# Delta rule and a rational mixture layer on one Trainium2 core: keys and queries transposed on TensorE in float32, weight words converted 768 at a time

## The chip, the core and the metric

The kernel runs on one core of one Trainium2 chip. The metric is the device time of one launch in microseconds (us). A core has five engines with an instruction stream each: TensorE (PE, the matmuls; PEld is its weight loads), VectorE (DVE), ScalarE (ACT), GpSimd (POOL) and SyncE (SP), which here does little but issue DMAs. Every engine works its stream in order and waits on semaphores for the others.

## What is computed

The reference first runs a delta rule over 768 tokens for 4 x 8 heads of width 48. After that every token's 384 values pass a two-layer network whose activation is a quotient of two polynomials.

```
k_n = k / (norm(k) + 1e-06)
for t in range(S):
    y[:, :, t] = q[t] @ state
    v_old = state @ k_n[t]
    state = state + beta[t] * outer(k_n[t], v[t] - v_old)
x = y, laid out as (B * S, H * D) = 3072 x 384
h = x @ w_in                                   # 384 x 2048
P = a0 + a1*h + a2*h^2 + a3*h^3
Q = 1 + |b0|*|h| + |b1|*h^2
out = (P / (Q + 1e-06)) @ w_out                # 2048 x 384
```

The two weight matrices come as float64, that is as pairs of 32-bit words, and are turned into float32 on the chip.

## The kernel before

**Chunks.** Tokens are worked in 12 chunks of 64 tokens (`C`, `NCH`). In a chunk the 32 sequences (4 batches times 8 heads) are held as two pairs (`PAIRS`) times two blocks of 64 partitions. Every float32 factor of a matmul is split into a float16 high part and a float16 rest (`split16`: ACT writes the high part, DVE or POOL subtracts it), and a product is three float16 passes (`PASSES`, `mm3`).

**A chunk's attention** is cut into steps that different chunks are in at the same time. `ahead` (L948) loads keys, values and queries with SP DMAs (`load`, L110) and normalizes the keys (`keys_normalized`, L486). `front` (L915) writes the transposed keys on the block diagonal of `kbd` (`keys_transposed`, L506), multiplies keys with keys (`key_products`, tile `pg`, L510), inverts 16 x 16 blocks on DVE (`inverse`, L523), scales and transposes the queries (L634) and multiplies them with the keys (`query_products`, tile `pm`, L649). `middle` (L932) fills the other block-diagonal operands by DMA (`to_diagonal`, L422; `diagonals`, L640). `back` (L888) solves (`pu`), updates the state with the keys in token order (`knbd`, product `pd`, L700) and makes the outputs (L711).

**Transposing before.** `transposed` (L448) splits 128 x 768 float32 values with ACT (L226) and POOL (L230) into the one buffer `kn`. Two DMAs (L458) write both parts to DRAM (`xdk`, `xdq`), padded from 48 to 64 values. A transposing DMA (L475) reads them back as `tk` or `tq`. Only chunk 0 (`soon`) transposes on TensorE, in float16 (L468, copies L470). For the state update, four DMAs (L428) read `xdk` out of DRAM again in runs of 128 bytes into `knbd`. `kbd` and `qbd` are filled from all 64 partitions, padding too (L433).

**Weights before.** `to_f32` (L309) makes float32 of 256 words (`load_in`, L329: three calls for each of 8 units) or 192 words (`load_out`, L347: four calls for each unit): a DMA into one of nine staging tiles of tags `mw`, `mu`, `mr`; ACT takes the absolute value of the high words (L316) into `wao` or `wai`; POOL clamps it (L317); DVE shifts (L318) and merges sign and low bits with two `scalar_tensor_tensor` (L325). The result is split into float16: in `load_in` on ACT and DVE, in `load_out` one half on ACT and DVE and the other half on POOL and ACT (L366 to L371).

**The layer** is a loop of 96 units (8 of each chunk): `hidden` (18 matmuls, L808), `numerator` (three ACT and three DVE instructions, L826 to L833), `quotient` (two ACT, three DVE, one POOL, L841 to L847) and `accumulate` (12 matmuls, L862). `attention` (L959) puts one step of four later chunks beside each unit.

**What sets the order.** A scheduler fixes each engine's stream before the run by a simulated time line. `tc.high_priority` lifts the recurrent steps, and the unit's DVE instructions keep their order (`in_order`, L794). Nearly all DMAs share the one SP queue. PSUM tiles rotate in pools: `ps_f` has one buffer, which `pg`, `pm`, `pe`, `pfq` and, from chunk 3 on, `px` take in turn.

Of the kernel before, what the change touches and what calls it, by code (L numbers as in the profile page):

```python
# [36 lines left out]
def kernel(  # L37
# [35 lines left out]
        "kn": [P, NPAIR, 2, H, 2, DP],  # L73
# [33 lines left out]
    LD_BUFS = {"k": 1, "q": 1, "v": 2}  # L107
    loaded = {}

    def load(nm, c):  # L110
        t = sb.tile([P, NPAIR * H, D], F32, tag="ld" + nm, name=f"{nm}_{c}", bufs=LD_BUFS[nm])
        with behind(nm, c):
            for b in range(2):
                sl, src = slice(b * C, (b + 1) * C), SRC[nm][:, :, c * C : (c + 1) * C]
                if nm == "v":
                    nc.sync.dma_start(out=t[sl], in_=src[2 * b : 2 * b + 2].rearrange("p h t d -> t (p h) d"))
                else:
                    for i in range(2):
                        nc.sync.dma_start(out=t[sl, i * H : (i + 1) * H], in_=src[2 * i + b].rearrange("h t d -> t h d"))  # L119
        loaded[nm, c] = t  # L120
# [64 lines left out]
    kn_b = zeroed(1, [P, 2, H, 2, DP], F16, "kn", lambda t: t[:, :, :, :, D:DP])[0]  # L185
# [123 lines left out]
    def to_f32(t, src, nm, keep=MIN_NORMAL):  # L309
# [6 lines left out]
        nc.scalar.activation(a, wh.bitcast(F32), AF.Abs)  # L316
        nc.gpsimd.tensor_scalar(a, a, 3.0e38, keep, op0=ALU.min, op1=ALU.max)  # L317
        nc.vector.tensor_scalar(  # L318
            t, a.bitcast(U32), 3, KEEP, op0=ALU.logical_shift_left, op1=ALU.bitwise_and
        )  # L320
        for word, scalar, in1, op0, op1 in (
            (wh, 0xC0000000, t, ALU.bitwise_and, ALU.bitwise_or),
            (wl, 29, t, ALU.logical_shift_right, ALU.bitwise_or),
        ):
            nc.vector.scalar_tensor_tensor(out=t, in0=word, scalar=scalar, in1=in1, op0=op0, op1=op1)  # L325
# [3 lines left out]
    def load_in(i):  # L329
        w64 = moe_w_in.bitcast(U32)  # L330
        t = w_out[:, i].rearrange("p a b e -> p (a b e)").bitcast(U32).rearrange("p (c f) -> p c f", c=NCC)
        for cc in range(NCC):
            to_f32(t[:, cc], w64[cc * P : (cc + 1) * P, i * 4 * P : (i + 1) * 4 * P], f"i{i}_{cc}")
        s2 = w_in[:, i, 0].bitcast(BF16)
        nc.scalar.activation(s2, t.bitcast(F32), AF.Square)
# [9 lines left out]
        split16((w_in[:, i, 0], w_in[:, i, 1]), t.bitcast(F32), sw[:, 0, i : i + 1])  # L345

    def load_out(i):  # L347
        w64 = moe_w_out.bitcast(U32)
        if i + 1 < NU:
            to = w_out[:, i + 1].rearrange("p a b e -> p a (b e)").bitcast(U32)  # L350
            to = [to[:, j] for j in range(2)]
        else:
            to = [staged([P, DM], U32, f"wo32_{i}_{j}") for j in range(2)]
        fs = sb.tile([P, 2], F32, tag="wfs", name=f"wfs_{i}")
        for j in range(2):
            f = 2 * i + j
            for e in range(2):
                cl = slice(e * DM // 2, (e + 1) * DM // 2)
                to_f32(to[j][:, cl], w64[f * P : (f + 1) * P, e * DM : (e + 1) * DM], f"o{f}_{e}", gate)
            sum_squares(fs[:, j : j + 1], to[j].bitcast(F32), w_out[:, i, 0, j])  # L360
        ss = sb.tile([P, 2], F32, tag="ss", name=f"vss_{i}")
        nc.vector.tensor_scalar(ss[:, 0:1], fs[:, 0:1], fs[:, 1:2], 2.0 ** -30, op0=ALU.add, op1=ALU.max)
# [677 lines left out]
```

## Time and profile before

| what | value |
|---|---|
| time, median of 3 runs | 843.59 us (839.91 to 846.07) |
| the profiled execution's own time | 849.25 us |
| its span from first to last instruction | 845.5 us |
| mean granted TensorE clock | 0.944 of full speed |
| DMA packets, bytes | 466507, 111.46 MB |
| first unit's DVE work (L830) starts | 150.29 us |
| starts of chunks 1, 2, 3, 4, 5 of the layer | 223.66, 296.13, 371.55, 428.05, 483.62 us |
| starts of chunks 6 to 11 | 544.97, 604.99, 664.30, 719.16, 764.19, 800.18 us |

The span is 3.75 us shorter than the execution's time, and that execution was 5.66 us above the median of the runs. An engine's busy time counts an instruction that stands blocked in its execution as busy. Rows that group instructions give the line of kernel.py, the engine, the operation, output and inputs with shapes, the count, the busy time with the mean of one in ns, and then the idle time ahead of them with what ended it. A row of a view by stretches gives the stretch, its length, each engine's busy time with the count of instructions, then the granted clock, the mean busy share of the 16 DMA engines and GB/s.

### The profile page before, as it was taken

What the parts mean: (1) busy time and instruction counts of PE and PEld (TensorE: products, weight loads), DVE (VectorE), ACT (ScalarE), POOL (GpSimd) and SP (SyncE); (2) the same over time, 40 slices, a digit from 0 to 9 for tenths busy, and PEclk for the clock granted to TensorE, in tenths of its full rate; (3) what the DMA queues carried; (4) which work ended last, traced back from release to release, by engine and by line L of the source; (5) the groups of instructions that cost most, each with busy time, mean ns of one, the idle gap of its engine ahead of it and who ended that gap; (6) DMA issues with size and microseconds to landing.
All of it is one profiled execution on the core that took longest, in us unless ns stands there. A gap on an engine that the chain in (4) does not pass through costs nothing.

```text
span 845.5 us, 23179 instructions
## 1 busy us (share of the span) xinstructions
PE 627.7 (74%) x9264; PEld 493.8 (58%) x9264; DVE 740.2 (88%) x1405; ACT 617.1 (73%) x1278; POOL 338.1 (40%) x322
## 2 busy tenths in 40 slices
PE   0330346778778777866978988789789789999995
PEld 0220344666566666755866866667567667786662
DVE  5999896688879778987998999989988799998996
ACT  4866658768667675866966968768668768788873
POOL 6545754334435333253433433432433332222232
PEclk9999996898989898989999999989899999999999
DMA  8998979769979879999599399696597674300000
GB/s 237 249 212 170 225 155 170 123 140 169 157 130 165 146 120 191 146 140 183 93 145 187 71 176 150 119 193 105 98 167 111 110 103 80 76 2 21 1 19 19
DMA packets 466507, 111.46 MB, mean 132 GB/s; under 512 B 431328, under 2 KB 463072, under 8 KB 466400
## 3 DMA queue, kind: packets, MB, share of 16 engines
q1 hardware_dynamic: 464224, 108.83, 71.3%
q8 instruction: 72, 1.18, 0.6%
q10 hardware_dynamic: 2176, 1.17, 0.5%
q14 instruction: 35, 0.29, 0.1%
HBM read 40.47 MB, written 26.23 MB: 79 GB/s over the span
## 4 chain that ended last, share of the span: by engine, by line
DVE 34%; PE 19%; DMA 17%; SPq 11%; ACT 10%; issue 7%; POOL 1%; ACTq 0%; DVEq 0%; POOLq 0%
PE ph L808 7%; PE po L862 5%; DVE ph L845 4%; DVE w_out L325 4%; DVE mg L844 3%; DVE mw L830 3%; DVE mu L833 3%; DVE mu L832 3%; SPq L119 3%; PE pu L401 2%; DMA tq<-xdq 2%; DMA gd<-g 2%; DMA tk<-xdk 2%; SPq L475 2%; DVE mu L846 2%
## 5 line engine op out<-in xcount | busy, mean ns | idle before, releaser
L862 PE MATMUL po<-w_out,mg 128*128 128x384 f16 x1152 | 226.5, 339 | 33.3 <-DVE mg L844 20.9
L847 POOL TENSOR_TENSOR mg<-mu,mr 128x512 f16<-128x512 f32 x96 | 124.8, 1300 | 258.1 <-DVE mu L846 203.8
L808 PE MATMUL ph<-xT,w_in 128*128 128x256 f16 x1728 | 216.3, 280 | 14.1 <-DVE mu L846 11.2
L808 PEld LDWEIGHTS <-w_in 128*128 128x128 f16 x1728 | 169.8, 101 | 51.1 <-DVE mu L846 14.4
L862 PEld LDWEIGHTS <-mg 128*128 128x128 f16 x1152 | 109.5, 101 | 103.4 <-DVE mg L844 27.7
L401 PEld LDWEIGHTS <-kbd 128*128 128x128 f16 x1680 | 66.7, 109 | 47.8 <-issue 43.3
L830 DVE SCALAR_TENSOR_TENSOR mw<-mr,msc,ph 128x512 f32<-128x512 f32 x96 | 71.1, 741 | 22.1 <-ACT mu L828 21.9
L831 ACT ACTIVATE mw<-mw 128x512 f32<-128x512 f32 x96 | 60.4, 629 | 39.7 <-DVE mw L830 39.2
L845 DVE SCALAR_TENSOR_TENSOR ph<-mw,msc,mg 128x512 f32<-128x512 f32 x96 | 81.4, 848 | 1.0
L844 DVE SCALAR_TENSOR_TENSOR mg<-mu,msc,mr 128x512 f16<-128x512 f32 x96 | 81.1, 844 | 0.0
L826 ACT ACTIVATE mr<-ph,msc 128x512 f32<-128x512 f32 x96 | 65.2, 679 | 18.7 <-PE ph L808 6.9
L828 ACT ACTIVATE mu<-ph,coef,msc 128x512 f32<-128x512 f32 x96 | 74.2, 773 | 0.0
L846 DVE SCALAR_TENSOR_TENSOR mu<-mu,msc,ph 128x512 f32<-128x512 f32 x96 | 71.1, 741 | 1.4
L833 DVE SCALAR_TENSOR_TENSOR mu<-mu,msc,ph 128x512 f32<-128x512 f32 x96 | 70.7, 736 | 1.0
L841 ACT ACTIVATE mr<-mw,msc 128x512 f32<-128x512 f32 x96 | 69.2, 721 | 1.7
L401 PE MATMUL pu<-z,ebd 128*128 128x48 f16 x1728 | 54.9, 185 | 18.1 <-DVE z L232 13.5
L401 PEld LDWEIGHTS <-ebd 128*128 128x128 f16 x1728 | 53.9, 98 | 21.7 <-issue 19.4
L832 DVE TENSOR_TENSOR mu<-ph,mu 128x512 f32<-128x512 f32 x96 | 65.5, 682 | 0.0
L842 ACT ACTIVATE mr<-mr 128x512 f32<-128x512 f32 x96 | 60.3, 628 | 1.3
L401 PEld LDWEIGHTS <-wbd 128*128 128x128 f16 x1152 | 37.7, 99 | 35.9 <-issue 34.8
L230 POOL TENSOR_TENSOR mm<-m,mm 128x1024 f16<-128x1024 f32 x12 | 29.2, 2436 | 73.6 <-ACT mm L226 64.5
L401 PE MATMUL pm<-tq,kbd 128*128 128x64 f16 x576 | 27.0, 220 | 20.1 <-DMA tq<-xdq 18.3
(195 smaller groups left out, 1195.0 us busy)
## 6 DMA issues: line engine op xcount, KB each, us to landing
wsi<-in_moe_w_in_dram SPq DMA_DIRECT2D x24, 256.0 KB, 5.0
xdk<-kn SPq DMA_DIRECT2D x24, 256.0 KB, 3.7
kbd<-tk SPq DMA_DIRECT2D x24, 256.0 KB, 5.5
gd<-g SPq DMA_DIRECT2D x24, 256.0 KB, 3.5
wso<-in_moe_w_out_dram SPq DMA_DIRECT2D x32, 192.0 KB, 3.9
xdq<-kn SPq DMA_DIRECT2D x24, 256.0 KB, 3.6
mbd<-mm SPq DMA_DIRECT2D x24, 256.0 KB, 5.5
wc<-img SPq DMA_DIRECT2D x24, 256.0 KB, 5.1
```

Source lines behind the costliest of these rows:

```text
L401: nc.tensor.matmul(dst[p][:, h], head(bd, lp, p * H + h), head(rt, rp, p * H + h), start=start and n == 0 and h == 0, stop=stop and n == l ...
L808: nc.tensor.matmul(ph[:, i], w_in[:, f2, wp, cc, i * P : (i + 1) * P], x[:, xp, cc], start=k == 0, stop=k == 3 * NCC - 1,)
L828: nc.scalar.activation(u, ph, AF.Identity, scale=A3, bias=a2)
L830: in_order(nc.vector.scalar_tensor_tensor(out=w, in0=z, scalar=B0, in1=ph, op0=ALU.add, op1=ALU.mult))
L832: in_order(nc.vector.tensor_mul(u, ph, u))
L833: in_order(nc.vector.scalar_tensor_tensor(out=u, in0=u, scalar=A1, in1=ph, op0=ALU.add, op1=ALU.mult))
L841: nc.scalar.activation(r, w, AF.Ln, bias=Q0)
L844: in_order(nc.vector.scalar_tensor_tensor(out=g[:, 0], in0=u, scalar=A0, in1=r, op0=ALU.add, op1=ALU.mult))
L845: in_order(nc.vector.scalar_tensor_tensor(out=t, in0=w, scalar=Q0, in1=g[:, 0], op0=ALU.add, op1=ALU.mult))
L846: in_order(nc.vector.scalar_tensor_tensor(out=u, in0=u, scalar=A0, in1=t, op0=ALU.add, op1=ALU.subtract))
L847: nc.gpsimd.tensor_mul(g[:, 1], u, r)
L862: nc.tensor.matmul(po[p], g[:, gp, i, p * P : (p + 1) * P], w_out[:, f2, wp, i], start=f2 == lo and i == 0 and k == 0, stop=f2 == hi - 1 a ...
```

## The change

1. `load` puts keys and queries into two fixed tiles `kw`, `qw` of [128, 8, 2, 64] float32 whose padding is zeroed once. One partition's heads lie as TensorE wants them.
2. `transposed` makes 8 TensorE transposes of 128 x 128 in float32 into one `ps_f` tile (`pt`). Then `split16` writes high part and rest from PSUM for each pair: two ACT copies and two DVE subtractions of 128 x 512. This holds for keys and queries of all 12 chunks. The DRAM rows, the transposing DMAs and the float16 transposes of chunk 0 are gone, and queries are no longer split in SBUF.
3. Keys for the state update are still split by ACT and POOL, in two halves of 384, into one of three tiles `kn` in SBUF, which four DMAs copy to `knbd` in runs of 256 bytes. Chunk 11 skips this.
4. `kbd` and `qbd` are filled from 48 partitions instead of 64.
5. `to_f32` takes 768 words at a time, 16 calls instead of 56, in place in its target. Staging is three tiles of tag `mx`; a unit's `u`, `w`, `r` share such a tile.
6. In `load_out` both halves of `w_out` are split together by ACT and DVE; POOL no longer scales or subtracts there.
7. `dynamic_dma_scratch_size=2048` is given to the program.

```diff
-        t = sb.tile([P, NPAIR * H, D], F32, tag="ld" + nm, name=f"{nm}_{c}", bufs=LD_BUFS[nm])
+        t = wide[nm] if nm in wide else sb.tile([P, HP, D], F32, tag="ld" + nm, name=f"{nm}_{c}", bufs=LD_BUFS[nm])
...
-    kn_b = zeroed(1, [P, 2, H, 2, DP], F16, "kn", lambda t: t[:, :, :, :, D:DP])[0]
+    kn_b = zeroed(3, [P, 2, 2, NH, DP, HG], F16, "kn", lambda t: t[:, :, :, :, D:DP], eng=nc.vector)
...
-        nc.sync.dma_start(out=st.rearrange("p f w -> p (f w)"), in_=src)
+        parts_ = src.shape[1]
+        nc.sync.dma_start(out=st.rearrange("p (a f) w -> p a (f w)", a=parts_), in_=src)
...
+        to_f32(t, w64[:, i * 4 * P : (i + 1) * 4 * P].rearrange("(c p) x -> p c x", p=P), f"i{i}")
...
-        for j in range(2):
-            if j == 0:
-                split16((w_out[:, i, 0, j], w_out[:, i, 1, j]), to[j].bitcast(F32), ss[:, 1:2])
-            else:
-                scaled(to[j].bitcast(F32), ss[:, 1:2])
-                split16((w_out[:, i, 0, j], w_out[:, i, 1, j]), to[j].bitcast(F32), eng=nc.gpsimd)
+        split16((w_out[:, i, 0], w_out[:, i, 1]), t, ss[:, 1:2])
...
             if nm == "kn":
-                for a in range(HG):
+                for p in PAIRS:
                     nc.sync.dma_start(
-                        out=bd[sl].rearrange("t p i (n a) b d -> t (p i n) a b d", a=HG)[:, :, a, b],
-                        in_=t[:, :, :, :, a, b].rearrange("p i n t d -> t (p i n) d"),
+                        out=bd[sl, p, :, :, b].rearrange("t i n d a -> t (i n) (d a)"),
+                        in_=t[p * C : (p + 1) * C, b].rearrange("t i n d a -> t (i n) (d a)"),
                     )
...
-    def transposed(x, src, nm, soon):
+    def transposed(x, nm):
+        t = sb.tile([P, NPAIR, 2, NH, C, HG], F16, tag="tt", name="t" + nm)
+        pt = ps_f.tile([P, H, P], F32, tag="a", name=f"pt{nm}")
+        for h in range(H):
+            nc.tensor.transpose(pt[:, h], x[:, h].rearrange("p b d -> p (b d)"), identf)
         for p in PAIRS:
+            split16(
+                [t[:, p, i].rearrange("x n t a -> x n a t") for i in range(2)],
+                pt[:, :, p * C : (p + 1) * C].rearrange("x (n a) t -> x n a t", a=HG),
             )
+        return t
...
+        if c + 1 < NCH:
+            kd = kn_b[c % 3]
+            for b in range(2):
+                split16(
+                    [kd[:, b, i, :, :D].rearrange("p n d a -> p n a d") for i in range(2)],
+                    kt[:, :, b].rearrange("p (n a) d -> p n a d", a=HG),
+                    eng=nc.gpsimd,
+                )
+        info[c] = {"tk": transposed(wide["k"], f"k_{c}"), "kd": kd}
...
-        scaled(qt, d["sq"])
-        d["tq"] = transposed(kn_b, qt, f"q_{c}", c == 0)[0]
+        scaled(qt[..., :D], d["sq"])
+        d["tq"] = transposed(qt, f"q_{c}")
```

The change also lets the scheduler write other streams. DVE before, where the words of `w_out` begin (`wso` is a staged block of words, `wao` the clamped magnitudes):

```order
L318 TENSOR_SCALAR w_out_135<-wao0_1_1113 128x192
L318 TENSOR_SCALAR w_out_135<-wao1_0_1122 128x192
L325 SCALAR_TENSOR_TENSOR w_out_135<-wso0_1_1111,w_out_135 128x192
L325 SCALAR_TENSOR_TENSOR w_out_135<-wso1_0_1120,w_out_135 128x192
L325 SCALAR_TENSOR_TENSOR w_out_135<-wso0_1_1111,w_out_135 128x192
L318 TENSOR_SCALAR w_out_135<-wao1_1_1130 128x192
L325 SCALAR_TENSOR_TENSOR w_out_135<-wso1_0_1120,w_out_135 128x192
L325 SCALAR_TENSOR_TENSOR w_out_135<-wso1_1_1128,w_out_135 128x192
```

And the same place of the change:

```order
L316 TENSOR_SCALAR w_out_143<-w_out_143 128x768
L286 TENSOR_SCALAR tab_145<-tab_145,coef_103 128x4
L235 SCALAR_TENSOR_TENSOR w_in_142<-w_out_143,sw_144,w_in_142 128x768
L318 SCALAR_TENSOR_TENSOR w_out_143<-wso1_968,w_out_143 128x768
L351 TENSOR_SCALAR vss_0_959<-wfs_0_957 128x1
L318 SCALAR_TENSOR_TENSOR w_out_143<-wso1_968,w_out_143 128x768
L316 TENSOR_SCALAR w_out_143<-w_out_143 128x768
L254 TENSOR_SCALAR sw_144<-lgw0_961 128x1
```

Three instructions of 768 now stand where twelve of 192 stood. Of the 48 subtractions of the new transposes 10 come ahead of the first unit (keys of chunks 0, 1, 2 and queries of 0, 1), 38 behind it.

SP before, one round of the loop (the queue that issues DMAs; `xdq`, `xdk` are the DRAM rows):

```order
L458 DMA xdq_5702<-kn_109 64x8x256 x2
L433 DMA qbd_117<-tq_4594 64x16x128 x2
L441 DMA mbd_125<-mm_4821 64x16x128
L475 DMA_TRANSPOSE tq_5705<-xdq_5702 128x2048
L458 DMA xdk_5950<-kn_109 64x8x256 x2
L884 DMA out_dram<-ob_5967 64x2x384 x2
L441 DMA mbd_125<-mm_4821 64x16x128
L475 DMA_TRANSPOSE tk_5953<-xdk_5950 128x2048
L587 DMA img_129<-wh_6163 128x16x16
```

And SP of the change, where `qbd` of the same chunk is filled:

```order
L423 DMA kbd_121<-tk_4499 48x16x128 x2
L569 DMA wc_4723<-img_139 64x16x64 x2
L496 DMA gd_5178<-g_5228 64x16x64 x2
L418 DMA knbd_127<-kn_117 64x8x128 x4
L506 DMA gb_5331<-gd_5178 128x16x16
L423 DMA qbd_125<-tq_4242 48x16x128 x2
L122 DMA qw<-in_q_dram 64x8x48
```

Six issues a chunk are gone, and `knbd` reads `kn` in SBUF. TensorE's stream of the change, with the transposes of the queries of chunk 8 (`ptq`) ahead of a unit's first matmuls (`ph`):

```order
L391 LDWEIGHTS knbd_127
L391 MATMUL pd_7899<-z_7896,knbd_127 128x48
L443 MATMUL ptq_7576<-identf,qw 128x128 x8
L786 LDWEIGHTS w_in
L786 MATMUL ph_7601<-xT_7107,w_in 128x256
```

Before, nothing stood between `pd` and the unit's matmuls there; now whatever the eight transposes wait for, the unit behind them waits for too.

More of the change, by code (lines that the diff above doesn't have):

```diff
@@ L106 @@
     SRC = {"k": k, "q": q, "v": v}
-    LD_BUFS = {"k": 1, "q": 1, "v": 2}
+    LD_BUFS = {"v": 2}
     loaded = {}
+    wide = {nm: cpool.tile([P, H, 2, DP], F32, name=nm + "w") for nm in "kq"}
+    for t in wide.values():
+        nc.vector.memset(t[:, :, :, D:], 0.0)
     def load(nm, c):
-        t = sb.tile([P, NPAIR * H, D], F32, tag="ld" + nm, name=f"{nm}_{c}", bufs=LD_BUFS[nm])
+        t = wide[nm] if nm in wide else sb.tile([P, HP, D], F32, tag="ld" + nm, name=f"{nm}_{c}", bufs=LD_BUFS[nm])
         with behind(nm, c):
@@ L349, in load_out @@
         if i + 1 < NU:
-            to = w_out[:, i + 1].rearrange("p a b e -> p a (b e)").bitcast(U32)
-            to = [to[:, j] for j in range(2)]
-        else:
-            to = [staged([P, DM], U32, f"wo32_{i}_{j}") for j in range(2)]
-        fs = sb.tile([P, 2], F32, tag="wfs", name=f"wfs_{i}")
-        for j in range(2):
[L356 to L360, printed above, removed]
+            t = w_out[:, i + 1].rearrange("p a b e -> p (a b e)").bitcast(U32)
+        else:
+            t = staged([P, 2 * DM], U32, f"wo32_{i}")
+        to_f32(t, w64[2 * i * P : (2 * i + 2) * P].rearrange("(j p) x -> p j x", j=2), f"o{i}", gate)
+        t = t.bitcast(F32).rearrange("p (j e) -> p j e", j=2)
+        fs = sb.tile([P, 1], F32, tag="wfs", name=f"wfs_{i}")
+        sum_squares(fs, t, w_out[:, i, 0])
         ss = sb.tile([P, 2], F32, tag="ss", name=f"vss_{i}")
-        nc.vector.tensor_scalar(ss[:, 0:1], fs[:, 0:1], fs[:, 1:2], 2.0 ** -30, op0=ALU.add, op1=ALU.max)
+        nc.vector.tensor_scalar_max(ss[:, 0:1], fs, 2.0 ** -30)
         ro = sw[:, 1, i : i + 1]
@@ L823, in numerator @@
         ph = d["ph"]
[L825 removed]
+        m = sb.tile([P, 3, 2, TG], F32, tag="mx", name=f"mx{n}", bufs=MB)
+        u, w, r = (m[:, i] for i in range(3))
+        z = r
         nc.scalar.activation(z, ph, AF.Abs, scale=B1)
[L827 removed]
         nc.scalar.activation(u, ph, AF.Identity, scale=A3, bias=a2)
[L829 removed]
         in_order(nc.vector.scalar_tensor_tensor(out=w, in0=z, scalar=B0, in1=ph, op0=ALU.add, op1=ALU.mult))
```

108 lines of the change are left out of this document (35 added, 73 removed).

## The prediction

> **What bounds the kernel now.** I read the page first, then the time by stretches, cut where the layer begins and at the chunks of it, then DVE's waits.
>
> ```profile
> PE 627.7 (74%) x9264; PEld 493.8 (58%) x9264; DVE 740.2 (88%) x1405; ACT 617.1 (73%) x1278; POOL 338.1 (40%) x322
> DVE 34%; PE 19%; DMA 17%; SPq 11%; ACT 10%; issue 7%; POOL 1%; ACTq 0%; DVEq 0%; POOLq 0%
> ```
>
> DVE is the busiest engine; 740.2 of 845.5 us leave it 105.3 us idle. Yet DMA and its queue hold 28% of the chain that ended last, so an edit of the DMAs can pay though DVE carries most of the work. By stretch, with DVE's busy time, the granted clock, the DMA share and GB/s:
>
> ```profile
> 0.00:150.30 150.30, 127.82 (x348) 0.95 0.91 201
> 150.30:223.70 73.40, 56.95 (x119) 0.88 0.80 144
> 223.70:296.10 72.40, 61.21 (x108) 0.88 0.90 152
> 296.10:371.60 75.50, 65.48 (x117) 0.93 0.89 148
> 371.60:428.10 56.50, 51.36 (x90) 0.94 0.80 139
> 483.60:545.00 61.40, 59.58 (x107) 1.00 0.90 147
> 764.20:800.20 36.00, 34.83 (x60) 1.00 0.05 13
> ```
>
> Three stages show. Ahead of the layer (to 150.3 us) DVE idles 22.5 us, part of it before the first data, while the DMA engines are 91% busy. In the next chunks each stretch holds 1.8 to 16.5 us of DVE idleness, at 80 to 90% DMA share. At 764 us nothing of attention is left, DMA is at 5%, and DVE idles 1.2 of 36 us: there it alone sets the pace. What ends DVE's idle time between 150 and 760 us (total, times, longest):
>
> ```profile
> DVE mw L830 <- ACT mu L828: 19.5, 14, 4.2
> DVE m L655 <- PE pm L401: 10.6, 5, 3.7
> DVE ab L545 <- DMA gb<-gd: 7.2, 6, 2.5
> DVE sc L617 <- PE pfq L247: 6.3, 3, 3.5
> DVE nrm L492 <- ACT sq L491: 5.2, 3, 2.0
> PE pm L401 <- DMA tq<-xdq: 18.3, 8, 4.8
> ACT kn L226 <- DMA xdq<-kn: 17.4, 7, 4.0
> ```
>
> The last two rows are for the whole span and tell what lies behind the first: TensorE stands before `pm` for the transposing DMA of the queries, and ACT stands because the single buffer `kn` is still being written out, so its layer instructions (`mu`) come late.
>
> **Weight words (gain ahead of the layer).** The conversion on DVE (mean ns of one; then, by line, shortest, median and longest):
>
> ```profile
> L325 DVE SCALAR_TENSOR_TENSOR w_out<-wso,w_out 128x192 uint32<-128x192 uint32 x56 | 24.3, 449 | 0.4
> L325 DVE SCALAR_TENSOR_TENSOR w_out<-wsi,w_out 128x256 uint32<-128x256 uint32 x48 | 21.8, 469 | 0.3
> L318 DVE TENSOR_SCALAR w_out<-wai 128x256 uint32<-128x256 uint32 x24 | 10.6, 441 | 4.7 <-POOL wai L317 4.7
> L318 DVE TENSOR_SCALAR w_out<-wao 128x192 uint32<-128x192 uint32 x28 | 10.4, 373 | 0.0
> L318 DVE TENSOR_SCALAR w_out<-wao x28: 234/249/1712, 74.2 to 121.1; 128x192 uint32<-128x192 uint32 x28
> L318 DVE TENSOR_SCALAR w_out<-wai x24: 274/284/1907, 18.3 to 62.4; 128x256 uint32<-128x256 uint32 x24
> L325 DVE SCALAR_TENSOR_TENSOR w_out<-wso,w_out x56: 322/357/1825, 74.5 to 124.9; 128x192 uint32<-128x192 uint32 x56
> L325 DVE SCALAR_TENSOR_TENSOR w_out<-wsi,w_out x48: 407/414/1629, 18.8 to 63.5; 128x256 uint32<-128x256 uint32 x48
> L232 DVE SCALAR_TENSOR_TENSOR w_in<-w_out,sw,w_in 128x768 f16<-128x768 f32 x8 | 8.7, 1083 | 0.0
> L232 DVE SCALAR_TENSOR_TENSOR w_out<-w_out,vss 128x384 f16<-128x384 f32 x7 | 5.0, 711 | 1.3 <-ACT w_out L228 0.7 <-ACT lgx L258 0.6
> ```
>
> The first four rows sum to 67.1 us; the last block's 8 merges and 4 shifts go to another tile, at the medians 8 x 0.357 + 4 x 0.249 = 3.9 us, together 71.0. Afterwards there are 16 shifts and 32 merges of 768. By the medians a shift grows 35 ns for 64 words, so 768 takes 284 + 8 x 35 = 564 ns; a merge grows 57 ns, so 414 + 8 x 57 = 870 ns, and the row of the same operation at 768 says 1083. I take 970 for it. That is 16 x (0.56 + 1.94) = 40.0 us, a gain of 31.0; with 0.90 and 1.08 it is 49 us and a gain of 22, with 0.87 one of 34.2. Against it `load_out` now subtracts 768 instead of 384 on DVE: 8 x (1.08 - 0.71) = +3.0 us.
>
> **New subtractions (loss on DVE).** The trace has no subtraction out of PSUM with output in steps of two. Neighbours:
>
> ```profile
> L832 DVE TENSOR_TENSOR mu<-ph,mu 128x512 f32<-128x512 f32 x96 | 65.5, 682 | 0.0
> L578 DVE SCALAR_TENSOR_TENSOR wh<-wt,wh 128x256 f16<-128x256 f32 x12 | 5.4, 453 | 0.0
> ```
>
> The first is the same size and source; the second, with output in such steps, is 10% above the median of its size (414). I take 700 ns, between 600 (rows of this kind overlap their successor by some 80 ns) and 800. The 10 ahead of the layer cost +7.0 us, the 38 behind +26.6 us (22.8 to 30.4). Nothing hides these: DVE is 84 to 97% busy in the stretches where they fall, except where a wait is removed.
>
> **DMA relief (gain in the layer).** Removed are 48 DRAM writes of 256 KB, 22 transposing DMAs of 0.5 MB and a quarter of `kbd` and `qbd`. One transposing DMA fills 232 to 237 us nearly alone, and two such writes with loads 228 to 230:
>
> ```profile
> 232.00:237.00 5.00, 1.00 1.13 137
> 228.00:230.00 2.00, 0.50 1.08 247
> ```
>
> So 22 x 5 + 12.6 MB / 247 GB/s = 110 + 51 = 161 us of full DMA work go, and six issues a chunk on SP. Of the waits, `m` goes whole (10.6 us). Of the other four, 38.2 us, I take half, 19.1, since only part of each is DMA (`ab` waits for one, `nrm` for the squares of loaded keys, `sc` for a matmul behind others). That is 29.7 us. TensorE's new place in front of a unit costs some of it back: I put 4 us. Net -26 us, between 0 (each wait finds another cause) and -45.
>
> The Trainium skill, page "Advanced Engine Details and Errata", section "X-Bar Transpose (TRN2)", speaks against this: transposing DMAs are as fast as regular ones. By it the 22 would have cost 2.1 us each at the 247 GB/s above, the relief would be 97 instead of 161 us, the net gain 16 and the result 10 us later. The row above, 5 us for 0.5 MB, does not bear it out; the 831 that it would give lies in the forecast's own range below.
>
> **What hides.** TensorE gets 192 float32 transposes, and ACT four copies a chunk for one cast:
>
> ```profile
> L745 PE MATMUL px<-identf,y 128*128 128x128 f32 x72 | 11.3, 298 | 0.8 <-DVE xs L739 0.8
> L470 ACT COPY tk<-ptk 128x512 f16<-128x512 f16 x4 | 2.6, 725 | 0.5 <-PE ptk L468 0.5
> L226 ACT CAST kn<-q 128x768 f16<-128x768 f32 x12 | 9.9, 826 | 0.1
> ```
>
> 8 transposes are 8 x 157 ns = 1.3 us, 19 times in the layer 24 us; ACT gains 4 x 0.725 - 0.83 = 2.1 us a chunk. Both lie in the idle quarter of these engines behind DVE; without that cover each is some 20 to 24 us. Edits 3, 4 and 7, the `mx` tiles and the smaller memsets I cost at nothing: the copies they touch land off DVE's path, a unit's three tiles were released by the same last reader (L847) before, and no row shows the scratch. POOL's leaving the queries frees a little of DVE's layer instructions that stand blocked beside it: -2 us.
>
> **Sum.** 849.25 - 31.0 + 3.0 + 7.0 + 26.6 - 26 - 2 = 826.8 us for an execution like the profiled one. The median of the runs stands at 843.59 / 849.25 = 0.9933 of that execution, so 821.3, say **821 us**.
>
> **Rivals.** *A larger gain ahead of the layer and in it.* DVE and POOL block each other, as this pair shows:
>
> ```profile
> 33.75 1.93 POOL L230 TENSOR_TENSOR gl<-g,gl 128x768 f16<-128x768 f32 x1 [0.48 <-ACT gl L226]
> 33.92 1.91 DVE L318 TENSOR_SCALAR w_out<-wai 128x256 uint32<-128x256 uint32 x1
> L317 POOL TENSOR_SCALAR wao<-wao,gate 128x192 f32<-128x192 f32 x32 | 19.7, 622 | 15.4 <-ACT wao L316 9.3 <-DVE gate L582 5.2 <-ACT sc L627 0.7
> L317 POOL TENSOR_SCALAR wai<-wai 128x256 f32<-128x256 f32 x24 | 12.4, 524 | 13.3 <-ACT wai L316 10.4 <-DVE sw L341 1.2 <-DVE wss L343 0.9
> L243 POOL TENSOR_SCALAR q<-q,sc x12: 903/909/1607, 41.7 to 660.3; 128x768 f32<-128x768 f32 x12
> L230 POOL TENSOR_TENSOR w_out<-w_out 128x384 f16<-128x384 f32 x7 | 6.8, 973 | 1.5 <-ACT w_out L226 1.5
> L243 POOL TENSOR_SCALAR w_out<-w_out,vss 128x384 f32<-128x384 f32 x7 | 5.0, 711 | 4.3 <-DVE vss L365 4.2
> ```
>
> A shift of 0.28 us took 1.91 while POOL subtracted. POOL's 32.1 us of clamping become about 16 x 0.91 = 14.6, by the median of its 768-wide scaling, and `w_out`'s 11.8 us for 7 units, 13.5 for 8, go: 31 us. If the two engines truly take turns there, the stretch shrinks by 31 instead of 21.0; if besides the five waits vanish whole (48.8 - 4), the sum is 849.25 - 31 + 26.6 - 44.8 - 2 = 798, as a median 793. For it: the first three chunks run at 73 us where later ones run at 56. Against it: later ones with as much DMA have waits too. The Trainium skill, page "SBUF — State Buffer", section "SBUF: two separate sides", calls the pair's shared port an exclusive lock held for the whole instruction; by it this would be the case ahead of the layer.
>
> *The waits only move.* DVE is the bound and idles as long as before: 849.25 - 21.0 + 26.6 - 2 = 852.9, as a median 847. For it: a stretch at 97% (483.6) has no idleness to give.
>
> *A new wait in TensorE's stream (slower).* Each of the 19 transposes in the layer stands ahead of a unit's matmuls and takes the one `ps_f` buffer until ACT and DVE, each busy with units, have emptied it. Priced as the wait it replaces, 18.3 / 8 = 2.3 us, all 19 are 44 us; with 29.7 removed this is 852.9 - 29.7 + 44 = 867.2, median 861. It decides from (849.25 - 823.2) / 19 = 1.4 us for each. Against it: the stream puts other matmuls between a transpose and the next user of `ps_f`.
>
> **Chances.** The forecast 0.45 (own range 806 to 838), the larger gain 0.20, moved waits 0.19, the new wait 0.16. Beyond 1% of 843.6 (835.2 and 852.0), which is about what a measurement here can tell from no change, faster takes most of the first, the second and a little of the third: 0.66. Within 1%: 0.17. Slower: 0.17. The range 790 to 852 reaches to the second case and past the third, and leaves out the fourth and the far end of the second.
>
> **What would show it.** Right: the first unit's DVE work near 130 us instead of 150.3, conversion rows of 38 to 49 us in sum, 48 subtractions of 0.6 to 0.8 us, DMA share in the layer near 0.6, no wait of `pm` on a DMA, and DVE's idle total near 80 us with busy time near 745. Wrong: TensorE waiting on POOL or ACT before `pt`, ACT or DVE waits for `pt` above 1 us each, chunks of the layer still at 70 us, or conversions as dear per word as before.

## The result and the profile after

The changed kernel takes 832.93 us (median of 4 runs, 828.52 to 836.82), the kernel before 844.83 us on the same chip: a ratio of 0.985, 95% interval 0.980 to 0.990: a gain of 1.5%, outside the spread of the runs but under 2%. The forecast was 821 us, with its range from 790 to 852. The profiled execution took 832.65 us, its span is 830.9 us. (The spans of the two profiled executions differ by 14.6 us, the medians by 11.9.) First the page, in the two rows that were read of before:

```profile
PE 636.0 (77%) x9424; PEld 508.1 (61%) x9424; DVE 748.3 (90%) x1338; ACT 632.0 (76%) x1252; POOL 299.3 (36%) x263
DVE 44%; PE 23%; DMA 11%; ACT 10%; issue 6%; SPq 3%; POOL 2%; POOLq 0%; ACTq 0%; DVEq 0%
```

DMA and SP's queue fell from 28% of the chain to 14%, and DVE took their place. DVE idles 82.6 us instead of 105.3; the forecast said busy near 745, idle near 80. Totals hide where that came from, so the same stretches again (DVE's busy time, granted clock, DMA share, GB/s):

```profile
0.00:150.86 150.86, 118.50 (x242) 0.67 0.76 168
150.86:220.18 69.32, 62.96 (x126) 0.94 0.71 105
220.18:292.00 71.82, 67.28 (x115) 0.95 0.62 112
292.00:358.87 66.87, 60.11 (x106) 0.95 0.63 114
358.87:418.14 59.27, 57.37 (x106) 0.97 0.63 105
473.86:532.47 58.61, 58.27 (x101) 1.00 0.60 107
748.84:785.39 36.55, 34.83 (x60) 1.00 0.05 12
```

The first row is the surprise: the first unit still starts at 150.86 us, before at 150.29. DVE has 9.3 us less to do there and idles 32.4 us instead of 22.5. All of the gain lies in the layer, 680.0 us instead of 695.2, where the DMA share fell to 0.6 to 0.7. DVE's and TensorE's waits there (150 to 765 us; total, times, longest):

```profile
DVE mx L808 <- ACT mx L807: 7.5, 8, 1.5
DVE sc L595 <- PE pfq L250: 4.9, 4, 2.3
DVE ab L523 <- DMA gb<-gd: 1.3, 2, 1.1
DVE nrm L467 <- ACT nrm L466: 1.0, 1, 1.0
PE ptk L443 <- DVE m L633: 2.1, 2, 1.5
PE pm L391 <- DVE et L235: 1.8, 3, 0.9
PE ptq L443 <- POOL qw L246: 0.9, 2, 0.7
```

The five waits that made 48.8 us before are 14.7 us (the first four rows; `m` behind `pm` is gone). The new transposes cost TensorE about 3 us of waiting in the whole layer. Ahead of it DVE waits 6.3 us for ScalarE's first part of the keys (`tk`), which it did not before; in all it idles 9.9 us longer there. What was converted and subtracted, by line (busy, mean ns of one):

```profile
L318 DVE SCALAR_TENSOR_TENSOR w_out<-wsi,w_out 128x768 uint32<-128x768 uint32 x16 | 18.1, 1132 | 0.1
L318 DVE SCALAR_TENSOR_TENSOR w_out<-wso,w_out 128x768 uint32<-128x768 uint32 x14 | 13.6, 975 | 0.0
L316 DVE TENSOR_SCALAR w_out<-w_out 128x768 uint32<-128x768 uint32 x15 | 9.6, 638 | 0.4 <-POOL w_out L315 0.4
L318 DVE SCALAR_TENSOR_TENSOR wo<-wso,wo 128x768 uint32<-128x768 uint32 x2 | 2.6, 1294 | 0.0
L316 DVE TENSOR_SCALAR wo<-wo 128x768 uint32<-128x768 uint32 x1 | 0.5, 542 | 0.0
L233 DVE TENSOR_TENSOR tk<-ptk,tk 128x512 f16<-128x512 f32 x24 | 17.5, 730 | 7.5 <-ACT tk L229 7.5
L233 DVE TENSOR_TENSOR tq<-ptq,tq 128x512 f16<-128x512 f32 x24 | 17.5, 729 | 0.4 <-ACT tq L229 0.4
L235 DVE SCALAR_TENSOR_TENSOR w_out<-w_out,vss 128x768 f16<-128x768 f32 x7 | 7.1, 1015 | 1.9 <-ACT w_out L231 1.8
```

The conversion is 44.4 us in sum (forecast 40, bounds 38 to 49; 71.0 before), the 48 subtractions 35.0 us (forecast 33.6). Nearly every price was right, and the end of the first stretch was not. The experiments ask why.

### The profile page after: what moved, and what is told of

It reads as the page before. It is cut to its first block, busy times and chain, and to the rows that moved or that the text cites. A ratio compares the mean times of both kernels' runs of the same rounds, so it can differ in the third digit from the quotient of the medians.

```text
span 830.9 us, 23153 instructions
## 1 busy us (share of the span) xinstructions
PE 636.0 (77%) x9424; PEld 508.1 (61%) x9424; DVE 748.3 (90%) x1338; ACT 632.0 (76%) x1252; POOL 299.3 (36%) x263
## 4 chain that ended last, share of the span: by engine, by line
DVE 44%; PE 23%; DMA 11%; ACT 10%; issue 6%; SPq 3%; POOL 2%; POOLq 0%; ACTq 0%; DVEq 0%
PE po L840 7%; PE ph L786 6%; DVE ph L823 6%; DVE mg L822 4%; DVE mx L808 4%; DVE mx L811 3%; DVE mx L810 3%; PE pu L391 3%; DVE mx L824 2%; DMA v<-in_v_dram 1%; DMA gb<-gd 1%; DVE tq L233 1%; DVE w_out L318 1%; DVE m L633 1%; DVE pr L544 1%
## 5 line engine op out<-in xcount | busy, mean ns | idle before, releaser
L825 POOL TENSOR_TENSOR mg<-mx 128x512 f16<-128x512 f32 x96 | 125.1, 1303 | 304.0 <-DVE mx L824 233.3
L823 DVE SCALAR_TENSOR_TENSOR ph<-mx,msc,mg 128x512 f32<-128x512 f32 x96 | 94.1, 980 | 0.8
L809 ACT ACTIVATE mx<-mx 128x512 f32<-128x512 f32 x96 | 60.4, 630 | 35.0 <-DVE mx L808 34.5
L808 DVE SCALAR_TENSOR_TENSOR mx<-mx,msc,ph 128x512 f32<-128x512 f32 x96 | 71.3, 742 | 11.6 <-ACT mx L807 9.0
L822 DVE SCALAR_TENSOR_TENSOR mg<-mx,msc 128x512 f16<-128x512 f32 x96 | 77.2, 804 | 0.0
L806 ACT ACTIVATE mx<-ph,msc 128x512 f32<-128x512 f32 x96 | 65.2, 679 | 13.7 <-PE ph L786 8.2
L807 ACT ACTIVATE mx<-ph,coef,msc 128x512 f32<-128x512 f32 x96 | 74.2, 773 | 0.0
L824 DVE SCALAR_TENSOR_TENSOR mx<-mx,msc,ph 128x512 f32<-128x512 f32 x96 | 71.1, 740 | 1.3
L811 DVE SCALAR_TENSOR_TENSOR mx<-mx,msc,ph 128x512 f32<-128x512 f32 x96 | 70.9, 739 | 0.7
L819 ACT ACTIVATE mx<-mx,msc 128x512 f32<-128x512 f32 x96 | 69.1, 720 | 1.7
L810 DVE TENSOR_TENSOR mx<-ph,mx 128x512 f32<-128x512 f32 x96 | 65.7, 684 | 0.0
L820 ACT ACTIVATE mx<-mx 128x512 f32<-128x512 f32 x96 | 60.3, 628 | 1.5
L231 ACT ACTIVATE z<-pu,zmask 128x768 f16<-128x768 f32 x36 | 32.3, 896 | 13.9 <-PE pu L391 13.9
```

The lines of the kernel that those rows point to most:

```text
L807: nc.scalar.activation(u, ph, AF.Identity, scale=A3, bias=a2)
L808: in_order(nc.vector.scalar_tensor_tensor(out=w, in0=z, scalar=B0, in1=ph, op0=ALU.add, op1=ALU.mult))
L810: in_order(nc.vector.tensor_mul(u, ph, u))
L811: in_order(nc.vector.scalar_tensor_tensor(out=u, in0=u, scalar=A1, in1=ph, op0=ALU.add, op1=ALU.mult))
L819: nc.scalar.activation(r, w, AF.Ln, bias=Q0)
L822: in_order(nc.vector.scalar_tensor_tensor(out=g[:, 0], in0=u, scalar=A0, in1=r, op0=ALU.add, op1=ALU.mult))
```

## The experiments

The theory (A in most runs): ahead of the layer a chain of solving steps, casts and transfers of the first chunks sets the first unit, so DVE's saving there turns into idle time, while the layer gains from the relief of the DMA engines. The rival (B): DVE's work sets both stretches, the conversion paid, and the transposes took it back. Times are medians; each ratio is against the kernel before on the same chip. "First unit" and "layer" come from each kernel's profiled execution.

### The two halves apart

`conv_only` is the kernel before with this part of the change (and with the joint split of `w_out` and the `mx` tiles):

```diff
-            to_f32(t[:, cc], w64[cc * P : (cc + 1) * P, i * 4 * P : (i + 1) * 4 * P], f"i{i}_{cc}")
+        to_f32(t, w64[:, i * 4 * P : (i + 1) * 4 * P].rearrange("(c p) x -> p c x", p=P), f"i{i}")
```

> The kernel before with the 768-word conversion alone (three tiles of mx instead of nine, one joint split of w_out); keys and queries still go through the transposing DMA. Theory A (the stretch ahead of the layer is set by a chain of transfers, SP's queue and attention steps, so that DVE's saving there turns into idle time): conversion rows near 44 us instead of 71, the first unit still at 147 to 154 us, the layer as long as before (690 to 700 us), the time 840 to 850. Theory B (the conversion earns its 20 us and the new transposes and subtractions of the change take them back ahead of the layer): first unit at 126 to 136 us, the time 820 to 830.

Measured 841.13 us, ratio 0.996 (0.992 to 0.999); first unit 146.6, layer 689.8. Theory A, with both stretches just under its numbers: DVE has 10.4 us less busy time ahead of the layer (117.4 instead of 127.8), and the first unit comes 3.7 us earlier.

`tr_only` is the changed kernel with the old pieces, the old split of `w_out` and nine staging tiles:

```diff
-        return sb.tile(shape, dtype, tag="mx", name=nm, bufs=MB)
+        stage[0] += 1
+        tag, bufs = STAGES[stage[0] % len(STAGES)]
+        return sb.tile(shape, dtype, tag=tag, name=nm, bufs=bufs)
```

> The changed kernel with the weight words converted in pieces of 256 and 192 through nine staging tiles, as before the change; the TensorE transposes and all else stay. Theory A (chain): first unit at 148 to 156 us, the layer 676 to 686 us as in the changed kernel, the time 828 to 840: nearly the whole of the change's gain is here. Theory B (the transposes lengthen the stretch, the conversion shortens it): first unit at 165 to 175 us, the time 846 to 856.

Measured 835.81 us, ratio 0.989 (0.985 to 0.992); first unit 155.2, layer 676.9. Theory A again. The halves add up: -0.4% and -1.1% are the -1.5% of the whole, and most of the layer's gain belongs to the transposes (18.3 us here, 5.4 in `conv_only`). But a part of theory B is true at about a fifth of its size. DVE has 6.1 us more to do ahead of the layer than before, and the first unit comes 4.9 us later; in the whole change the conversion's 4 us and the transposes' 5 us cancel.

### Ahead of the layer: what does DVE's work there cost?

`no_conv` leaves out the shift and the merges of every weight piece:

```diff
-        nc.vector.tensor_scalar(t, t, 3, KEEP, op0=ALU.logical_shift_left, op1=ALU.bitwise_and)
-        for word, scalar, op0 in ((wh, 0xC0000000, ALU.bitwise_and), (wl, 29, ALU.logical_shift_right)):
-            nc.vector.scalar_tensor_tensor(out=t, in0=word, scalar=scalar, in1=t, op0=op0, op1=ALU.bitwise_or)
```

> The changed kernel without DVE's three instructions for each weight piece (the shift and the two merges, some 44 us of DVE); ScalarE's magnitude and POOL's clamp stay, so the weights have wrong values. Theory A (ahead of the layer the first chunk's chain of solving steps and transfers sets the first unit): first unit at 135 to 147 us, the time 816 to 832. Theory B (DVE's work sets it, and something else took the saving): 44 us of work less bring the first unit to 105 to 120 us, the time to 785 to 805.

Measured 826.25 us, ratio 0.978 (0.973 to 0.982); first unit 136.4, layer 687.8: theory A. Its first stretch (columns: length; PE, PEld, DVE, ACT, POOL busy; clock; DMA share; GB/s):

```profile
0.00:136.40 136.40, 48.74 (x691) 42.39 (x691) 77.77 (x194) 93.65 (x202) 52.17 (x66) 0.77 0.78 179
```

DVE idles 58.6 of 136.4 us, and still the first unit does not come before 136. DVE's busy time is not the pace there. Taking it away returns about a third: 3.7 us for 10.4 (`conv_only` against before), 4.3 for 15.4 (the change against `tr_only`), 14.5 for 40.7 here. Another order moves the first unit as much: in `kbd_dve` (below) it comes 6.9 us earlier with 4.1 us more DVE work ahead of it.

ScalarE's steps of chunk 0 show where the time goes: three casts of `z` in the solving steps, the last cast, and the output `y`. Before, then after, then `no_conv` (count: shortest, median, longest ns, first and last start):

```profile
L228 ACT ACTIVATE z<-pu,zmask x3: 882/882/890, 101.0 to 113.5; 128x768 f16<-128x768 f32 x3
L226 ACT CAST z<-pu x1: 789/789/789, 119.3 to 119.3; 128x768 f16<-128x768 f32 x1
L718 ACT ACTIVATE y<-py,sc x1: 883/883/883, 131.6 to 131.6; 128x768 f32<-128x768 f32 x1
```

```profile
L231 ACT ACTIVATE z<-pu,zmask x3: 882/900/901, 93.7 to 112.2; 128x768 f16<-128x768 f32 x3
L229 ACT CAST z<-pu x1: 798/798/798, 117.4 to 117.4; 128x768 f16<-128x768 f32 x1
L696 ACT ACTIVATE y<-py,sc x1: 908/908/908, 127.5 to 127.5; 128x768 f32<-128x768 f32 x1
```

```profile
L231 ACT ACTIVATE z<-pu,zmask x3: 901/901/901, 92.6 to 103.6; 128x768 f16<-128x768 f32 x3
L229 ACT CAST z<-pu x1: 787/787/787, 108.4 to 108.4; 128x768 f16<-128x768 f32 x1
L693 ACT ACTIVATE y<-py,sc x1: 904/904/904, 117.1 to 117.1; 128x768 f32<-128x768 f32 x1
```

The transposes on TensorE bring the first solving step from 101.0 to 93.7 us (93.0 in `tr_only`, 100.4 in `conv_only`); leaving the conversion out brings it no further than 92.6. The three starts of `z` lie 12.5 us apart in all before, 18.5 after and 11.0 without conversion. DVE's steps of the chain stand behind weight pieces there, and these are longer now (1.1 us instead of 0.45); that this stretches them is argued from the order.

The solving steps alone do not set the first unit, though. The 7.3 us that the changed kernel is ahead at the first `z` shrink to 1.9 at the last cast and 4.1 at `y`. After `y`, small steps of DVE and ScalarE in turn (`kp`) compute the scales of chunk 0, and `msc`, their product with the weights' scales, is what ScalarE's first instruction of the first unit waits for in the changed kernel. DVE's first step of `kp` and its `msc` (start and duration in us), before, after, `no_conv`:

```profile
137.54 0.21 DVE L758 RECIPROCAL kp<-lgx 128x1 f32<-128x1 f32 x2
146.56 0.18 DVE L787 TENSOR_TENSOR msc<-tab,sf 128x24 f32<-128x24 f32 x1 [1.06 <-ACT sf L761]
136.53 0.21 DVE L736 RECIPROCAL kp<-lgx 128x1 f32<-128x1 f32 x2
149.20 0.18 DVE L765 TENSOR_TENSOR msc<-tab,sf 128x24 f32<-128x24 f32 x1
123.94 0.21 DVE L733 RECIPROCAL kp<-lgx 128x1 f32<-128x1 f32 x2
134.22 0.68 DVE L762 TENSOR_TENSOR msc<-tab,sf 128x24 f32<-128x24 f32 x1 [1.06 <-ACT sf L736]
```

Between the two it is 9.0 us before, 12.7 after and 10.3 in `no_conv`; 9.0 in `conv_only`, 17.0 in `tr_only`, 19.7 in `k16` (below), whose `y` at 116.6 is earlier than that of `no_conv` while its first unit is at 145.0. So the changed kernel, 1.0 us ahead at `kp`, is 2.6 us behind at `msc`; before, the first unit starts 3.7 us after `msc`, after the change 1.7. In its trace, pieces of 0.7 to 1.0 us (the new subtractions `tk`, the values `v`, the splitting of `w_out`) run on both engines between steps of 0.15 to 0.4 us. No run moved these pieces, so that they are the cause is not shown.

`actq` asks whether SP's queue holds that chain, where weight loads wait for one of three staging tiles:

```diff
-        nc.sync.dma_start(out=st.rearrange("p (a f) w -> p a (f w)", a=parts_), in_=src)
+        nc.scalar.dma_start(out=st.rearrange("p (a f) w -> p a (f w)", a=parts_), in_=src)
```

> The changed kernel with the 16 transfers of the weight words issued from ScalarE's queue instead of SP's, so that the transfers of attention no longer stand behind a weight transfer that waits for one of three staging tiles. Theory A (SP's queue holds the chain ahead of the layer): first unit 8 to 15 us earlier, at 136 to 143 us, the time 818 to 826. Theory B (the chain's own steps set the stretch, the queue does not): first unit at 148 to 154 us, the time 829 to 837; if ScalarE stands for staging tiles in its turn, later than that.

Measured 847.08 us, ratio 1.003 (1.000 to 1.007); first unit 154.3, layer 687.4. My theory A, that SP's queue holds the chain, fell: with the weights out of it the first unit is later, as the last case of theory B allowed. How much of that is ScalarE standing for staging tiles was not separated.

### The layer: which part of the relief pays?

`dma_back` puts the traffic back, with nobody waiting for its result:

```diff
+            for p in PAIRS:
+                nc.sync.dma_start(
+                    out=xd[p].rearrange("i n t a b d -> t (i n) (a b d)"),
...
+            nc.sync.dma_start(out=junk, in_=xd.rearrange("p i n t a b d -> (p i n t a) (b d)"), transpose=True)
```

> The changed kernel, in which each transposed tile but the first two is also written to DRAM (two transfers of 256 KB) and read back by a transposing DMA into a tile that nobody uses: the traffic and the issues on SP of before, without anyone waiting for their result. Theory A (the layer's gain is relief of the DMA engines and of SP's queue): the DMA share in the layer goes back to 0.8 to 0.9, the layer to 692 to 702 us, the time to 842 to 855. Theory B (the gain is that no matmul waits for the transposed rows any more, and the traffic is hidden): the layer 678 to 684 us, the time 828 to 838.

Measured 858.33 us, ratio 1.018 (1.012 to 1.023); first unit 149.6, layer 706.8. Theory A, beyond the upper end of its numbers, though the DMA share over the whole layer is 0.62 and not the 0.8 to 0.9 that I wrote (0.50 in the changed kernel). DVE's busy time is that of the changed kernel (746.2 to 748.3), so all of the 25.4 us is idleness: no instruction needs these rows, but they stand in the way of other transfers, on the DMA engines or in SP's queue. The main DMA queue's row, before, after and here (packets, MB, share of 16 engines' span):

```profile
q1 hardware_dynamic: 464224, 108.83, 71.3%
```

```profile
q1 hardware_dynamic: 356128, 81.69, 53.5%
```

```profile
q1 hardware_dynamic: 425120, 104.76, 64.1%
```

As shares of their spans these are 602.8, 444.5 and 549.0 us of full DMA work. The change removed 158 us (forecast 161). The 22 transposing DMAs and 44 of the 48 writes, put back, are 104.5 us of it and cost 25.4 us.

`dma_free` is the same, with the transposing DMA reading a fixed tile, so that SP does not stand for the two writes ahead of it:

```diff
-            nc.sync.dma_start(out=junk, in_=xd.rearrange("p i n t a b d -> (p i n t a) (b d)"), transpose=True)
+            nc.sync.dma_start(out=junk, in_=xfix.rearrange("p i n t a b d -> (p i n t a) (b d)"), transpose=True)
```

> As the run with the traffic put back, but the transposing DMA reads a fixed DRAM tile that is written once at the start, so that SP's queue does not stand for the two writes of the rows ahead of it; traffic and issues are the same. Theory A (the DMA engines' load itself delays the other transfers): the time 850 to 860 as there. Theory B (SP's queue, standing for the written rows, delays the transfers behind it): the time 832 to 842.

Measured 864.75 us, ratio 1.025 (1.019 to 1.030); layer 713.4. Theory A, above its numbers, and not better than `dma_back` but worse (the profiled execution, with this layer, lay 5.6 us above its median). Standing for these rows alone does not explain the cost. That it is the DMA engines' load is not shown either: SP stands 45.0 us at the added transfers here, for tiles that are not finished or not free, and 31.2 us in `dma_back`.

`poolload` takes loads out of SP's queue:

```diff
-                nc.sync.dma_start(out=t[sl], in_=src[2 * b : 2 * b + 2].rearrange("p h t d -> t (p h) d"))
+                nc.gpsimd.dma_start(out=t[sl], in_=src[2 * b : 2 * b + 2].rearrange("p h t d -> t (p h) d"))
```

> The changed kernel with the 120 loads of keys, queries and values issued from POOL's queue instead of SP's. Theory A (the load on the DMA engines, not the order of SP's queue, delays the transfers): the time 828 to 840. Theory B (transfers of attention stand behind these loads in SP's queue): the layer 8 to 15 us shorter, the time 817 to 826. If POOL stands for a buffer while units wait for its products: above 840.

Measured 890.84 us, ratio 1.051 (1.044 to 1.058); first unit 170.9. Far above both theories' numbers, as the last sentence allowed: POOL is busy 380.1 us instead of 299.3. So it says nothing about SP's queue.

### What do the subtractions cost?

`no_sub` writes only the first part of each transposed tile (`tts` are two tiles zeroed once):

```diff
-            split16(
-                [t[:, p, i].rearrange("x n t a -> x n a t") for i in range(2)],
+            nc.scalar.copy(
+                t[:, p, 0].rearrange("x n t a -> x n a t"),
```

> The changed kernel without the 48 subtractions of the transposed tiles: the second part of transposed keys and queries stays zero, so the matmuls run as before on less exact data. Theory A (the layer is set by DVE, where each of its 0.73 us counts): the layer 20 to 28 us shorter (652 to 660 us), the first unit 2 to 5 us earlier, the time 801 to 812. Theory B (the subtractions lie in DVE's idle time): the layer at most 8 us shorter, the time 822 to 832.

Measured 822.81 us, ratio 0.973 (0.968 to 0.978); first unit 146.7, layer 677.3. Theory B's range: 35 us of rows gone (21.6 us of DVE's busy time) give 10 us.

`dbl_sub` does each subtraction twice:

```diff
+            nc.vector.tensor_sub(lo, src, hi)
```

> The changed kernel with each of the 48 subtractions of the transposed tiles done twice (the second writes the same result again): 35 us more of DVE, 5 to 8 of them ahead of the layer. Theory A (DVE is not the pace of the layer; its work there is hidden for the most part, as leaving the subtractions out gave 10 us of 35): the time 835 to 846. Theory B (the idle time is used up, and each further microsecond of DVE counts): the time 855 to 868.

Measured 863.74 us, ratio 1.022 (1.019 to 1.025); first unit 151.6, layer 709.8. Theory B's range: 31 us for 35 us of rows. But DVE's busy time grew by 15.9 us only, since other rows became shorter (those of L823 by 20.4 us), and its idle time by 14.6. The two runs contradict each other as prices of one instruction, so the scheduler's order must be looked at. `no_conv`, `actq` and `k16` (below) have nearly the changed kernel's work in the layer, and their layers are 687.8, 687.4 and 686.2 us long instead of 680.0. Another order alone moves it by 6 to 8 us.

`sub_cheap` therefore keeps the order: after the streams are fixed, each subtraction is replaced in its place by a cheaper instruction:

```diff
+    def cheap(i):
+        return MUL[0].__replace__(
+            name=i.name,
+            outs=[flat(i.outs[0])],
+            ins=[flat(i.ins[1]), mybir.ImmediateValue(dtype=F32, value=2.0 ** -14)],
+            sync_info=i.sync_info,
+        )
```

> The changed kernel, every instruction of each engine in its place, but with the 48 subtractions of the transposed tiles replaced by a DVE multiplication of the first part by 2 to the power of -14 (128 x 512 float16 in SBUF, estimate 0.25 to 0.40 us from a copy of 2048 such elements that took 0.90 us; the second part has wrong values). This takes 16 to 23 us from DVE with the order kept, which the runs without and with twice the subtractions could not do. Theory A (at the changed kernel's balance DVE's work and the chain of attention hold the layer together, so that taking DVE work away gives little): the time 825 to 833, a gain of at most 8 us. Theory B (each microsecond of the subtractions counts, as the run with twice as many says, and the run without them was held back by another order): 809 to 819.

Measured 830.45 us (6 runs), ratio 0.984 (0.980 to 0.987): 2.5 us under the changed kernel, whose interval overlaps. The replaced rows:

```profile
L575 DVE TENSOR_SCALAR tk<-tk 128x512 f16<-128x512 f16 x24 | 13.2, 550 | 7.9 <-ACT tk L467 7.9
L575 DVE TENSOR_SCALAR tq<-tq 128x512 f16<-128x512 f16 x24 | 8.0, 335 | 0.8 <-ACT tq L467 0.7
```

13.8 us left these rows (35.0 to 21.2; my estimate was 16 to 23) and 19.0 us DVE's busy time. A fifth of the rows at most came off the time: the medians differ by 2.5 us, the ratios by 0.1%. (The profiled spans differ by 6.9, but this profiled execution was the fastest of the six.) Theory A: at this balance work taken from DVE gives little. Why `dbl_sub` costs so much is open; its stream is another one.

### Two ways on

`k16` transposes the keys' two float16 parts, which POOL splits anyway, and copies them on ScalarE:

```diff
+                nc.tensor.transpose(pts[:, i, h], kd[:, i, h // HG, :, :, h % HG].rearrange("p b d -> p (b d)"), ident16)
```

> The changed kernel with the keys transposed in float16, as the two parts that POOL has split for the state's keys anyway (16 float16 transposes instead of 8 of float32, and four copies on ScalarE instead of two casts there and two subtractions on DVE); queries as in the changed kernel. 24 subtractions, 17.5 us, leave DVE, 24 copies of about 0.73 us go to ScalarE. Theory A (DVE sets the layer, ScalarE has room): the layer 8 to 14 us shorter, the time 819 to 827. Theory B (ScalarE's copies come late and hold a chain as long as the subtractions did): the time 829 to 838.

Measured 834.58 us, ratio 0.987 (0.983 to 0.992); layer 686.2. Theory B: DVE lost 8.8 us of busy time, ScalarE gained 14.0, the time stayed.

`kbd_dve` fills `kbd` with copies on DVE instead of transfers:

```diff
-                dma = nc.sync.dma_start(
-                    out=bd[sl, :, :, :, b][:D].rearrange("x p i n t a -> x (p i n) (t a)"),
-                    in_=t[sl][:D].rearrange("x p i n t a -> x (p i n) (t a)"),
+                nc.vector.tensor_copy(
+                    bd[sl, :, :, :, b][:D].rearrange("x p i n t a -> x (p i n) (t a)"),
+                    t[sl][:D].rearrange("x p i n t a -> x (p i n) (t a)"),
```

> The changed kernel with the 24 transfers of 192 KB that put the transposed keys on the diagonal of kbd replaced by 24 copies of 48 partitions x 2048 float16 on DVE (estimate 0.6 to 1.2 us each, 14 to 29 us in all). Theory A (transfers and their landing times of about 5 us set the layer, DVE's work is mostly hidden): the layer 5 to 15 us shorter, the time 818 to 829. Theory B (DVE's work counts in full): the time 840 to 855.

Measured 830.54 us, ratio 0.983 (0.979 to 0.987); first unit 144.0, layer 684.1. Between the two theories, and not to be told from the changed kernel:

```profile
L423 DVE COPY kbd<-tk 48x2048 f16<-48x2048 f16 x24 | 21.6, 902 | 0.2
```

DVE is busy 23.2 us longer at no cost in time. Either the transfers that it spares were worth about as much, or added work is as cheap here as `sub_cheap` says of work removed; the two were not separated. Chunk 0's last `z` starts at 107.5 instead of 117.4 us. No run beat the changed kernel by more than its uncertainty with the computation whole.

## Why the prediction was right, and where it was wrong

The direction and the range held; the forecast was 12 us too low. By its own steps:

- **Weight words: the step that failed.** It took 31.0 us of rows (26.6 measured), 7.0 of new subtractions (7.3) and 3.0 in `load_out` (2.5), and moved the first unit by their sum, 21.0 us. The first unit did not move. Two links broke. First, rows of consecutive DVE instructions overlap: the groups of that stretch add up to 148.9 us before for 127.8 of busy engine, 133.0 and 118.5 after, in both some 60 ns for each instruction. 120 fewer instructions of this kind return 7 us of the rows' gain, and DVE's busy time fell by 9.3 us where the rows fell by 15.9. I had named this overlap for the subtraction and not taken it off the conversion. Second, busy time there is not the pace: `no_conv` took the whole conversion away and gained 14.5 us of 44, with DVE idle for 43% of the stretch. What the changed kernel's first unit waits for last are chunk 0's scales (`msc`), at the end of a path through DVE and ScalarE. The conversion earned 3 to 4 us of time (`conv_only` against before, the change against `tr_only`).
- **New subtractions.** The size was right: 38 in the layer are 27.7 us in rows, and all rows of the layer grew by 24.8 (forecast 24.6 with POOL's -2). "Nothing hides these" was wrong: DVE's busy time grew by 17.5 us, and at a fixed order making them cheaper gave 2.5 of 13.8. That the idleness which the relief left took them in is argued, not shown.
- **DMA relief.** Right that it pays, and somewhat too small in sum. Forecast 29.7 us of waits less 4 of new ones, 26 net; the rows show 34.1 and 3 to 5, and DVE's idle time in the layer fell by 32.6 us. `dma_back` shows that the traffic costs time though nobody waits for it; whether on the DMA engines or in SP's queue is open. The DMA work, 161 us forecast and 158 in the rows, agrees by luck. The 158 hold the 3.0 MB less of `kbd` and `qbd` and the longer runs of `knbd`, which the forecast's sum left out, and the measure itself moves: `conv_only` has 25.7 us less of it than the kernel before, for the same 108.83 MB. The transposing DMAs and writes that `dma_back` puts back are 104.5 us, where the forecast's prices give 157. Its 5 us for one transposing DMA look too much. In the kernel before, at 234 to 236 us inside the row it read, the engines count as 1.09 and 1.07 busy at only 33 and 18 GB/s. In `dma_back` SP issues one such DMA at 642.1 to 644.3 us and nothing more until 650.6:

```profile
643.00:644.00 1.00, 1.00 (x18) 0.99 (x15) 0.71 (x1) 1.00 (x3) 0.00 (x0) 1.00 0.52 99
644.00:645.00 1.00, 1.00 (x9) 0.61 (x7) 1.00 (x3) 1.00 (x3) 0.42 (x1) 1.00 1.27 270
645.00:646.00 1.00, 1.00 (x10) 0.80 (x9) 1.00 (x1) 1.00 (x2) 1.00 (x1) 1.00 0.74 164
```

  That is 2.5 us of full work for 0.53 MB; 22 times that, with the 44 writes at the forecast's 247 GB/s, would be 102 us. By the Trainium skill, page "Advanced Engine Details and Errata", section "X-Bar Transpose (TRN2)", transposing is as fast as plain copying, which at those 247 GB/s gives an estimate of 2.1 us each. This row is nearer to the page than to the forecast.
- **What hides.** The rows of the transposes are 30 us of TensorE, with a few us of waits; the slower rival needed 1.4 us at each of 19 and found 3 us in all.
- **The rivals.** The larger gain fell with its premise: POOL's busy time ahead of the layer went from 86.3 to 62.7 us and the stretch stayed. By the Trainium skill, page "SBUF — State Buffer", section "SBUF: two separate sides", DVE and POOL lock each other out, and single rows agree: L823's 96 instructions of the layer take 94.1 us here and 73.7 in `dbl_sub`; 18 of them take more than 1 us here and 2 there, each beside a POOL instruction. Ahead of the layer the stretch did not follow POOL. The moved waits came true ahead of the layer alone, where DVE idles 9.9 us longer; in the layer the waits went.

So the forecast held by two errors of opposite sign: 21.6 us too much gain ahead of the layer (0.6 lost instead of 21.0 won) and 13.8 too little in it (15.2 instead of 1.4: DVE's busy time grew by 7.1 us less than forecast, and its idle time fell by 6.6 us more). That they nearly cancel is luck. About half of the 12 us that are left is the factor for the median: the profiled execution of before lay 5.66 us above its median, that of the changed kernel 0.3 below.

## What to carry to other kernels

Before a saving on the busiest engine is booked, ask of that very stretch whether its end is set by that engine or by a chain that only passes through it: an experiment that removes the work altogether (`no_conv`) tells the most that can be had. Rows of short instructions overlap, so a sum of rows promises more than busy time can give. And transfers that nobody waits for are not free: 104.5 us of DMA work with its issues, which raised the DMA share of the layer from 0.50 to 0.62, cost 25 us here.

## What the runs showed of the hardware

- **The clock.** In the changed kernel TensorE's granted clock was 0.50 from 50 to 100 us and 0.67 over the first stretch; before it was 1.00 and 0.95. It did not visibly decide the time. `kbd_dve` had 0.66 there and its first unit at 144.0, `conv_only` 0.97 and 146.6, but these differ in more than the clock. Within `tr_only`, three executions with a mean clock of 0.95 to 0.96 took 831.64 to 836.83 us, six at 0.91 took 833.26 to 837.75. The rows (length; PE, PEld, DVE, ACT, POOL busy; clock; DMA share; GB/s), after and then before:

```profile
50.00:75.00 25.00, 4.11 (x33) 2.36 (x30) 24.28 (x49) 13.78 (x31) 11.04 (x7) 0.50 0.73 160
75.00:100.00 25.00, 7.54 (x141) 6.99 (x142) 19.75 (x40) 13.60 (x27) 4.07 (x4) 0.50 0.75 171
```

```profile
50.00:75.00 25.00, 6.13 (x65) 4.51 (x64) 24.08 (x67) 17.42 (x41) 9.39 (x11) 1.00 0.84 190
75.00:100.00 25.00, 7.10 (x145) 6.77 (x146) 22.70 (x67) 16.05 (x47) 17.31 (x27) 1.00 1.02 197
```

- **Issues on POOL.** 120 loads issued there are 87.1 us of POOL's rows, 0.73 us each, and its busy time grew by 80.8 us.
- **Float16 on DVE.** A multiplication of 128 x 512 float16 in SBUF took 284 ns in the queries' place and 286 in the keys' (medians); the means are 335 and 550, since single ones took up to 1.00 and 2.37 us. The longest, at 283.51 us, ran while POOL subtracted 128 x 1024 (`mm`, 283.32 to 285.74). The subtraction from PSUM took 730 on average in both.
